# Raw FFN weights loaded two tiles ahead, the first maximum of v behind the first score tile, and the value products as one block with a priority of its own

## The chip, the cores and the metric

The kernel runs on one core of one Trainium2 chip. Five engines work side by side, each through its own queue in order: PE (TensorE, matmuls), DVE (VectorE), ACT (ScalarE), POOL (GpSimd) and SP (SyncE), which here issues all DMA transfers. The metric is device time in microseconds of one execution, the median of three runs; lower is better.

## The reference, cut to what matters

Attention in which a query sees only the keys of its own cluster, and behind it a feed-forward network (FFN) whose hidden layer is the maximum of three products. B = 4 batches, H = 8 heads, S = 768 positions, D = 64, 16 clusters; the FFN has 3072 tokens, 512 inputs and 768 hidden units. Its weights come as 8-byte floats.

```python
q_assign = np.argmax(np.einsum('bhsd,hcd->bhsc', q_n, c_n), axis=-1)
k_assign = np.argmax(np.einsum('bhsd,hcd->bhsc', k_n, c_n), axis=-1)
mask = q_assign[:, :, :, None] == k_assign[:, :, None, :]
scores = scale * np.matmul(q, k.transpose(0, 1, 3, 2))
scores = np.where(mask, scores, -1000000000.0)
scores = scores - np.max(scores, axis=-1, keepdims=True)
attn = np.exp(scores)
attn = attn / (np.sum(attn, axis=-1, keepdims=True) + 1e-09)
attn_out = np.matmul(attn, v)
...
x = attn_out.transpose(0, 2, 1, 3).reshape(B * S, H * D)
h = np.maximum(np.maximum(x @ w1, x @ w2), x @ w3)
return h @ w_out
```

## The kernel before

**Steps, visits, rounds.** The work is cut into 192 score steps: one step is one head and one block of 128 queries against all 768 keys. Six steps make a visit: a pair of heads and a group `gi` of three query blocks. Four visits, one for each pair of heads, make a round of 24 steps; two rounds make a batch. Steps 0 to 23 are the first round of batch 0.

**A score step** (`scores`, lines 477 to 496): four matmuls on PE (L482, L484), the row maximum on DVE (L487), the exponential on ACT (L490), a half-precision high part on ACT (L493) and a low part (L495, on DVE in even steps and on POOL in odd ones), and a DMA transpose issued by SP (L496), which writes the tile `pt`. The PSUM tiles `big` have three buffers, shared by scores, value products and cluster scores.

**The value products of a visit** (`av`, lines 500 to 530): first the row sums are inverted (L504 on ACT, L505 on DVE) and spread over the partitions by 12 small matmuls (L510); then come 36 matmuls of the transposed attention tiles with v (L514), in turn for the first and the second head of the pair; then the division, and a split into high and low half precision (`xs`, `x16`, L522 to L529).

**The FFN of a round** (`ffn_units`) begins three steps into the next round: 18 hidden units of 12 matmuls each (L555), then three output units of 18 matmuls each (L589), which stand under the steps 24, 25 and 26 behind the round's end. They need the weights in half precision: `w16` (six column tiles of w1, w2, w3) and `wo16`.

**The weights** are made in the first two rounds. There are 24 raw tiles of 512 KB: three for each of the six column tiles (`w_units`) and six of w_out (`wo_units`). `convert` (lines 189 to 201) takes a buffer `wd` (two of them), has SP load the raw tile (L195), casts its upper words on ACT (L197) and joins the rest on DVE (L199). Before the load, `hold` (lines 118 to 120) has POOL copy one element of the latest row sum of the exponentials (`pace`) into the buffer, so that the load waits for that exponential. For each column tile follow a maximum (L225), a scale and three splits (L208 to L210, or L205 and L206); `common` scales w_out once, at the end.

**v.** For batch 0 all of v is loaded at the start in two tiles `vf` of 768 KB. Their maxima on DVE (L314) give one scale, and `v_prep` splits v pair by pair. The first of the two maxima stands ahead of the cluster rows of the first pair, behind the low part of q and k (`behind("lo", ...)`); the second comes with the first steps.

**What sets the order.** A planner orders the instructions of each engine when the program is built, on a modelled clock: of those that are ready in the model it takes the one with the lowest priority number, and it puts in all semaphores. `at_prio` sets that number from a step number; `spread` hands units out over a range of steps, with an offset that moves their number (`W_LATE` = -2, `F_LATE` = 0, `AV_LATE` = 2, `PREP_LATE` = -9). `tc.issue_after(x)` adds no wait: it only places instructions behind x in the queue of x's engine. `behind("nm", ...)` places units behind the latest row maximum on DVE, `behind("pe", ...)` behind the latest score matmul on PE. A visit's `av` is traced one step after the next visit has begun, with the number of the visit's end + 2.

Of the kernel before, what the change touches and what calls it, by code (L numbers as in the profile page):

```python
# [8 lines left out]
F32 = mybir.dt.float32  # L9
# [3 lines left out]
I16 = mybir.dt.int16  # L13
# [11 lines left out]
def kernel(  # L25
# [90 lines left out]
    pace = []  # L116

    def hold(x):
        if pace:
            nc.gpsimd.tensor_copy(x, pace[-1])  # L120

# [67 lines left out]
    def convert(wp, src, a, d):  # L189

        n = d.shape[-1]
# [3 lines left out]
        nc.sync.dma_start(out=xf[:, 1 : 1 + 4 * n].rearrange("p (a m) -> p a m", a=a), in_=src)  # L195
        up = top[0]
        nc.scalar.copy(up.bitcast(F16).rearrange("p (n w) -> p n w", w=2)[:, 0:n, 1], x[:, 1:, 0].bitcast(BF16))  # L197
        low = x[:, 0:n, 2:4].bitcast(I32).rearrange("p n w -> p (n w)")
        nc.vector.scalar_tensor_tensor(  # L199
            d.bitcast(I32), low, 13, up[:, 0:n], op0=ALU.logical_shift_right, op1=ALU.bitwise_or  # L200
        )
# [10 lines left out]
    def w_units(wp, jt):  # L212
# [4 lines left out]
        def load(i):  # L217
            def f():
                if not i:
                    got["x"] = wp.tile([P, 3 * n], F32, tag="wf", name="wf", bufs=2)  # L220
                w = (w1, w2, w3)[i].bitcast(I16).rearrange("(c p) n -> p c n", p=P)
                src = w[:, :, 4 * jt * P : 4 * (jt + 1) * P]
                convert(wp, src, CT, got["x"][:, i * n : (i + 1) * n])
# [21 lines left out]
        return [load(i) for i in range(3)] + [scale] + [split(i) for i in range(3)]  # L245

    def wo_units(fp):
        got = []

        def part(jt):  # L250
            def f():
                wp = fp[0]
                w = w_out.bitcast(I16)[jt * P : (jt + 1) * P, :]
                if jt % 3 == 0:
                    got[:] = [wp.tile([P, 3 * DM], F32, tag="wf", name="wf", bufs=2)]
                x = got[0][:, jt % 3 * DM : (jt % 3 + 1) * DM]
                convert(wp, w.rearrange("p (a n) -> p a n", a=1), 1, x)
# [27 lines left out]
        return [part(jt) for jt in range(JT)] + [common]  # L285
# [22 lines left out]
    def v_max_first():  # L308
        def part(i):
            def f():  # L310
                x = v_first[i] = fp[0].tile([P, 2 * S], F32, tag="vf", name="vf", bufs=2)
                h = H // 2
                nc.sync.dma_start(out=x, in_=vv[0, :, i * h : (i + 1) * h].rearrange("p h t d -> p (h t d)"))
                nc.vector.tensor_reduce(  # L314
                    vmax[:, 0, i : i + 1], x, axis=AX.X, op=ALU.max, apply_absolute_value=True
                )
# [160 lines left out]
    def scores(b, h, qt, pt, g, rs, by_pool):  # L477
# [12 lines left out]
        nc.scalar.activation(x, e, AF.Exp, bias=nm, scale=-1.0, accum_out=r)  # L490
        pace[:] = [r[0:1]]
# [8 lines left out]
    def av(b, pr, gi, pts, rs):  # L500

        v = v16[b, pr]
        t = big()
        nc.scalar.activation(rs, rs, AF.Copy, bias=1.0e-9)  # L504
        nc.vector.reciprocal(rs, rs)  # L505
        for g in range(G):
            at = 512 + g * P
            for i in range(2):
                w = rs[:, g, i : i + 1].broadcast_to([P, D])
                nc.tensor.matmul(t[D * i : D * i + D, at : at + P], w, ident, start=True, stop=True)  # L510
        parts = [(kt, a, c) for a, c in ((0, 0), (1, 0), (0, 1)) for kt in range(QT)]
        for n, (kt, a, c) in enumerate(parts):
            for i in range(2):
# [6 lines left out]
                )  # L520
        xs = sb.tile([P, NB], F32, tag="xs", name="xs", bufs=1)
# [88 lines left out]
    V_0, W_0 = 2, 2  # L610


# [7 lines left out]
    W_A, W_B, W_O = (3, 27), (25, 37), (33, 47)  # L620
    AV_LAG = 2
    PREP_LATE = -9
    W_LATE, F_LATE, AV_LATE = -2, 0, 2
# [22 lines left out]

    c_sb = load_centroids()
# [6 lines left out]
    behind("lo", vm[0])  # L654
    first[5]()
    wa = [u for j in range(JA) for u in w_units(fp[0], j)]

    def unpaced(u):
        p = pace[:]
        pace.clear()  # L660
        behind("nm", u)
        pace[:] = p

    spread([lambda u=u: unpaced(u) for u in wa[:W_0]], 0, 0)
    spread([lambda u=u: behind("nm", u) for u in prep_units(0, 1)], 0, 3, -4)
    spread([lambda u=u: behind("nm", u) for u in vm[1:]] + [lambda: v_prep(0, 0, True)], 0, 4, 0)
    spread(prep_units(0, 2), 4, 9, -4)
    spread(prep_units(0, 3), 10, 15, -4)
    spread([open_late], LATE, LATE)
    for pr in range(1, NPAIR):  # L670
        spread([lambda pr=pr: v_prep(0, pr, True)], pr * V - V_0, pr * V, 0)

    spread(wa[W_0:], *W_A, W_LATE)
    spread([u for j in range(JA, JT) for u in w_units(fp[0], j)], *W_B, W_LATE)
    spread(wo_units(fp), *W_O, W_LATE)
# [23 lines left out]
    for b, pr, gi in visits:  # L699
# [9 lines left out]
        u = lambda a=(b, pr, gi, pts, rs): behind("pe", av, *a)  # L709
        plan.setdefault(step + AV_LAG - 1, []).append((step + AV_LATE, u))  # L710
# [38 lines left out]
```

## Time and profile before

| | us |
|---|---|
| median of 3 runs | 871.94 (867.68 to 874.14) |
| the profiled execution's own time | 872.91 |
| its span, first to last instruction | 871.1 |

The page lists busy times by engine, a chain of work followed back from the last instruction, and groups of instructions by source line; L487 is line 487 of the kernel printed above. "a <-b" after a group's or a wait's name is what ended the wait. In lists of waits the three numbers are the total in us, the number of waits and the longest one. In timelines they are the start and the length in us. PEld is TensorE's weight load, which runs beside the matmuls; SPq is SP's queue. Consecutive matmuls overlap, so the end of one row of PE can lie behind the start of the next one.

### The profile page before, as it was taken

How to read it: one execution, taken by the hardware profiler on the slowest of the kernel's cores; microseconds unless marked ns; L12 is line 12 of the kernel's file. 1: busy time of each engine (PE TensorE's matmuls, PEld its weight loads, DVE VectorE, ACT ScalarE, POOL GpSimd, SP SyncE). 2: the span in 40 equal slices, each digit the busy share in tenths (PEclk: the TensorE clock that was granted, in tenths of full speed). 3: DMA queues.
4: the chain of work that ended last, by engine and by line, in shares of the span. 5: the costliest groups of instructions: out<-in, count | busy, mean ns of one | idle time of the engine just before them, and what ended most of it. 6: DMA issues, size and time to landing. Idle time of an engine off the chain costs nothing.

```text
span 871.1 us, 13288 instructions
## 1 busy us (share of the span) xinstructions
PE 729.3 (84%) x4629; PEld 391.6 (45%) x4629; DVE 559.7 (64%) x1169; ACT 463.1 (53%) x827; POOL 450.4 (52%) x464
## 2 busy tenths in 40 slices
PE   2035374788868989999789999997999999999997
PEld 0012132344434545555444555454545554555563
DVE  7663877786897867547686686368768663556110
ACT  2545467654663646646554656464556465566201
POOL 1166355658585565337655745266666652354221
PEclk9976566689888999999999999999999999999999
DMA  6176869986786778768888978597986976666300
GB/s 230 36 169 140 201 143 214 203 182 139 178 204 128 171 167 154 138 117 165 170 157 201 188 139 142 113 180 144 189 194 128 156 136 134 112 118 110 91 1 36
DMA packets 329154, 128.90 MB, mean 148 GB/s; under 512 B 304384, under 2 KB 315520, under 8 KB 329088
## 3 DMA queue, kind: packets, MB, share of 16 engines
q1 hardware_dynamic: 329088, 128.06, 71.5%
q8 instruction: 36, 0.59, 0.3%
q14 instruction: 30, 0.25, 0.1%
HBM read 31.49 MB, written 6.29 MB: 43 GB/s over the span
## 4 chain that ended last, share of the span: by engine, by line
PE 45%; DVE 18%; POOL 11%; DMA 10%; issue 9%; ACT 5%; SPq 1%; POOLq 0%; DVEq 0%; ACTq 0%
PE one L555 17%; PE one L589 11%; PE big L514 7%; DVE big L487 4%; PE big L482 4%; PE big L484 3%; POOL hl L495 3%; DMA pt<-hl 2%; DMA stage<-in_qk_dram 2%; PE big L510 2%; DMA wd<-in_moe_w_dram 2%; DMA wd<-in_moe_w_out_dram 2%; POOL qk L399 2%; DMA stage<-in_v_dram 2%; DVE hl L495 2%
## 5 line engine op out<-in xcount | busy, mean ns | idle before, releaser
L487 DVE TENSOR_SCALAR_CACHE_REDUCE big<-big,nsc 128x768 f32<-128x768 f32 x192 | 194.2, 1017 | 78.3 <-PE big L484 77.1
L495 POOL TENSOR_TENSOR hl<-e,hl 128x768 f16<-128x768 f32 x96 | 159.0, 1656 | 148.9 <-ACT hl L493 147.3
L555 PE MATMUL one<-x,w16a 128*128 128x384 f16 x1152 | 208.1, 330 | 5.1 <-DVE vf_h L567 3.7
L490 ACT ACTIVATE big<-big,nm 128x768 f32<-128x768 f32 x96 | 83.8, 873 | 146.3 <-DVE big L487 130.9
L555 PEld LDWEIGHTS <-w16a 128*128 128x128 f16 x1152 | 111.1, 98 | 90.0 <-issue 21.1
L482 PE MATMUL big<-qk 128*128 128x512 f16 (+1 forms) x384 | 105.9, 357 | 48.5 <-DVE hl L495 14.0
L514 PE MATMUL big<-pt,v 128*64 128x384 f16 x1152 | 129.8, 341 | 2.4 <-DMA pt<-hl 2.4
L490 ACT ACTIVATE e<-big,nm 128x768 f32<-128x768 f32 x96 | 86.5, 901 | 71.3 <-DVE big L487 56.4
L495 DVE TENSOR_TENSOR hl<-big,hl 128x768 f16<-128x768 f32 x96 | 91.4, 952 | 41.8 <-ACT hl L493 39.6
L555 PE MATMUL one<-x,w16b 128*128 128x384 f16 x576 | 108.3, 340 | 6.7 <-DVE vf_h L567 5.2
L484 PE MATMUL big<-qk 96*128 96x512 f16 (+1 forms) x384 | 106.5, 357 | 6.9 <-DVE qk L465 4.3
L514 PEld LDWEIGHTS <-v 128*64 128x64 f16 x1152 | 71.8, 114 | 50.9 <-issue 26.0
L482 PEld LDWEIGHTS <-qk 128*128 128x128 f16 x384 | 35.6, 102 | 104.8 <-issue 67.2
L493 ACT CAST hl<-e 128x768 f16<-128x768 f32 x96 | 80.1, 834 | 2.4 <-DMA pt<-hl 0.6
L555 PEld LDWEIGHTS <-w16b 128*128 128x128 f16 x576 | 57.5, 101 | 51.3 <-issue 17.5
L493 ACT CAST hl<-big 128x768 f16<-128x768 f32 x96 | 76.6, 798 | 2.0
L528 POOL TENSOR_SCALAR x<-xs 128x384 f16<-128x384 f32 x32 | 16.4, 512 | 99.3 <-DVE xs L524 83.8
L484 PEld LDWEIGHTS <-qk 96*128 96x128 f16 x384 | 40.4, 105 | 40.0 <-issue 9.2
L589 PE MATMUL one<-wo,wf_h 128*128 128x512 f16 x216 | 56.0, 381 | 0.8 <-ACT o L598 0.8
L589 PE MATMUL one<-wo,vf_h 128*128 128x512 f16 x216 | 51.8, 380 | 2.7 <-DVE vf_h L567 2.4
L367 DVE TENSOR_REDUCE q_m<-stage 128x1 f32<-128x768 f32 x32 | 30.2, 948 | 33.9 <-DMA stage<-in_qk_dram 33.8
L399 POOL TENSOR_TENSOR qk<-stage,qk 128x768 f16<-128x768 f32 x30 | 49.6, 1667 | 3.1 <-ACT qk L398 2.9
(150 smaller groups left out, 892.5 us busy)
## 6 DMA issues: line engine op xcount, KB each, us to landing
stage<-in_qk_dram SPq DMA_DIRECT2D x32, 384.0 KB, 5.0
wd<-in_moe_w_dram SPq DMA_DIRECT2D x18, 512.0 KB, 4.8
out_dram<-o SPq DMA_DIRECT2D x24, 256.0 KB, 2.5
qk<-qk SPq DMA_DIRECT2D x15, 384.0 KB, 4.3
qk<-qk SPq DMA_DIRECT2D x30, 192.0 KB, 3.4
stage<-in_v_dram SPq DMA_DIRECT2D x12, 384.0 KB, 4.6
pt<-hl SPq DMA_TRANSPOSE x192, 4.0
wd<-in_moe_w_out_dram SPq DMA_DIRECT2D x6, 512.0 KB, 4.5
```

Of the source, the lines that this page charges most:

```text
L367: nc.vector.tensor_reduce(m2[:, i : i + 1], x, axis=AX.X, op=ALU.max, apply_absolute_value=True)
L399: last["lo"] = nc.gpsimd.tensor_tensor(t[:, AQ, i], x, t[:, BQ, i], op=ALU.subtract)
L482: nc.tensor.matmul(t[:, lo:hi], aq[:, qs], ak[:, lo:hi], start=True, stop=False)
L484: last["pe"] = nc.tensor.matmul(t[:, lo:hi], bq[0:K2, qs], bk[0:K2, lo:hi], start=False, stop=True)
L487: last["nm"] = nc.vector.tensor_scalar(e, e, nsc[b, h // 2], 3.0e38, op0=ALU.mult, op1=ALU.min, accum_out=nm)
L490: nc.scalar.activation(x, e, AF.Exp, bias=nm, scale=-1.0, accum_out=r)
L493: nc.scalar.copy(hl[:, 0, :], x)
L495: eng.tensor_tensor(hl[:, 1, :], x, hl[:, 0, :], op=ALU.subtract)
L510: nc.tensor.matmul(t[D * i : D * i + D, at : at + P], w, ident, start=True, stop=True)
L514: nc.tensor.matmul(t[D * i : D * i + D, 0:NB], v[:, i, kt, a], pts[i][:, :, c * QT + kt, :], start=(n == 0), stop=(n == len(parts) - 1),)
L555: nc.tensor.matmul(t[:, 0:NB], w16[jt // JA][:, jt % JA, wa, i, ct], x16[b, gi, ct][:, xa, :], start=(n == 0), stop=(n == 3 * CT - 1),)
L589: nc.tensor.matmul(t[:, 0:DM], h16[jt][:, ha, tt * P : (tt + 1) * P], wo16[0][:, jt, wa, :], start=(n == 0), stop=(n == 3 * JT - 1),)
```

## The change

`convert` falls into `w_load` (buffer and DMA) and `w_convert` (cast and join); `hold` and `pace` go. The 24 raw tiles are numbered in order, six column tiles first, then w_out, and tile n has the nominal step k = 2 + 1.9 (n - 2). Its load stands at k - 1, its conversion at k + 1, and the scale and splits of a column tile at k + 2 to k + 5 of its third raw tile. Each of these units is traced behind the latest row maximum, exponential and transpose (`paced`), with a number two steps earlier. The first two raw tiles are loaded at the start, ahead of and behind the second pair's q and k and the two tiles of v. The scale of w_out moves to step 47.

The two maxima of v follow behind the row maximum of step 1, their scale behind that of step 2. The preparation of the third and fourth pair of heads stands at steps 2 to 7 and 7 to 13 (before: 4 to 9 and 10 to 15), behind the latest row maximum.

`av` falls into `av_sums` (the inverted row sums and their 12 matmuls), `av` (the 36 products) and `x_split`. They are still traced one step after the next visit has begun. Sums and split keep the number of the visit's end + 2; the products have the visit's end - 4.

```diff
-        x = wp.tile([P, n + 1, 4], I16, tag="wd", name="wd", bufs=2)
-        hold(x[0:1, 0, 0:2].bitcast(F32))
...
+    def w_load(wp, src, a, n):
+        x = wp.tile([P, n + 1, 4], I16, tag="wd", name="wd", bufs=2)
...
+    def w_convert(x, d):
...
-        return [part(0), part(1), sc]
+        return [lambda: load(0), lambda: load(1), part(0), part(1), sc]
...
+    def paced(step, u, keys=("nm", "exp", "dma"), late=-2):
+
+        def f():
+            with ExitStack() as st:
+                for k in keys:
+                    st.enter_context(tc.issue_after(last[k].ins))
+                u()
+
+        plan.setdefault(max(int(step // 1), 0), []).append((step + late, f))
...
-    behind("lo", vm[0])
+    wl[0]()
     first[5]()
...
+    second = prep_units(0, 1)
+    second[0]()
+    vm[0]()
+    vm[1]()
+    wl[1]()
+
+    W_STEP = 1.9
+    for n in range(24):
+        k = 2 + (n - 2) * W_STEP
+        if n >= 2:
+            paced(k - 1, (wl + ol)[n])
+        paced(max(k + 1, 0.5), (wc + oc)[n])
+        if n < 18 and n % 3 == 2:
+            for i, u in enumerate(wu[n // 3][2]):
+                paced(k + 2 + i, u)
+    paced(47, w_common)
+    spread([lambda u=u: behind("nm", u) for u in second[1:]], 0, 3, -4)
+    spread([lambda u=u: behind("nm", u) for u in vm[2:]] + [lambda: v_prep(0, 0, True)], 1, 4, 0)
+    spread([lambda u=u: behind("nm", u) for u in prep_units(0, 2)], 2, 7, -4)
+    spread([lambda u=u: behind("nm", u) for u in prep_units(0, 3)], 7, 13, -4)
...
-        u = lambda a=(b, pr, gi, pts, rs): behind("pe", av, *a)
-        plan.setdefault(step + AV_LAG - 1, []).append((step + AV_LATE, u))
+        k = step + AV_LAG - 1
+        plan.setdefault(k, []).extend(
+            [
+                (k + 1, lambda a=(b, pr, gi, rs): behind("pe", av_sums, *a)),
+                (k - 5, lambda a=(b, pr, gi, pts): behind("pe", av, *a)),
+                (k + 1, lambda a=(b, pr, gi): x_split(*a)),
+            ]
+        )
```

More of the change, by code (lines that the diff above doesn't have):

```diff
@@ L112, in pow2_scale @@
         return p, s
[L116 to L120, printed above, removed]
     last = {}
@@ L218, in f, with conv @@
             def f():
+                w = (w1, w2, w3)[i].bitcast(I16).rearrange("(c p) n -> p c n", p=P)
+                got[i] = w_load(wp, w[:, :, 4 * jt * P : 4 * (jt + 1) * P], CT, n)
+            return f
+        def conv(i):
+            def f():
                 if not i:
                     got["x"] = wp.tile([P, 3 * n], F32, tag="wf", name="wf", bufs=2)
-                w = (w1, w2, w3)[i].bitcast(I16).rearrange("(c p) n -> p c n", p=P)
-                src = w[:, :, 4 * jt * P : 4 * (jt + 1) * P]
-                convert(wp, src, CT, got["x"][:, i * n : (i + 1) * n])
+                w_convert(got.pop(i), got["x"][:, i * n : (i + 1) * n])
                 if i == 2:
@@ L243, in split, with load, f @@
             return f
-        return [load(i) for i in range(3)] + [scale] + [split(i) for i in range(3)]
+        return [load(i) for i in range(3)], [conv(i) for i in range(3)], [scale] + [split(i) for i in range(3)]
     def wo_units(fp):
         got = []
+        raw = {}
+        def load(jt):
+            def f():
+                w = w_out.bitcast(I16)[jt * P : (jt + 1) * P, :]
+                raw[jt] = w_load(fp[0], w.rearrange("p (a n) -> p a n", a=1), 1, DM)
+            return f
         def part(jt):
             def f():
-                wp = fp[0]
-                w = w_out.bitcast(I16)[jt * P : (jt + 1) * P, :]
                 if jt % 3 == 0:
-                    got[:] = [wp.tile([P, 3 * DM], F32, tag="wf", name="wf", bufs=2)]
+                    got[:] = [fp[0].tile([P, 3 * DM], F32, tag="wf", name="wf", bufs=2)]
                 x = got[0][:, jt % 3 * DM : (jt % 3 + 1) * DM]
-                convert(wp, w.rearrange("p (a n) -> p a n", a=1), 1, x)
+                w_convert(raw.pop(jt), x)
                 row = worow[:, jt : jt + 1]
@@ L283, in common @@
             wsc["w"], wsc["o"] = pw, po
-        return [part(jt) for jt in range(JT)] + [common]
+        return [load(jt) for jt in range(JT)], [part(jt) for jt in range(JT)], common
     vmax = cpool.tile([P, B, NPAIR], F32, name="vmax")
@@ L308, in v_max_first, with load @@
     def v_max_first():
+        def load(i):
+            x = v_first[i] = fp[0].tile([P, 2 * S], F32, tag="vf", name="vf", bufs=2)
+            h = H // 2
+            nc.sync.dma_start(out=x, in_=vv[0, :, i * h : (i + 1) * h].rearrange("p h t d -> p (h t d)"))
         def part(i):
             def f():
-                x = v_first[i] = fp[0].tile([P, 2 * S], F32, tag="vf", name="vf", bufs=2)
-                h = H // 2
-                nc.sync.dma_start(out=x, in_=vv[0, :, i * h : (i + 1) * h].rearrange("p h t d -> p (h t d)"))
+                x = v_first[i]
                 nc.vector.tensor_reduce(
@@ L489, in scores @@
         r = rs[:, g, (h & 1) : (h & 1) + 1]
-        nc.scalar.activation(x, e, AF.Exp, bias=nm, scale=-1.0, accum_out=r)
-        pace[:] = [r[0:1]]
+        last["exp"] = nc.scalar.activation(x, e, AF.Exp, bias=nm, scale=-1.0, accum_out=r)
         hl = sb.tile([P, 2, S], F16, tag="hl", name="hl", bufs=4)
@@ L498, with av_sums @@
     x16 = {}
-    def av(b, pr, gi, pts, rs):
-        v = v16[b, pr]
-        t = big()
+    av_out = {}
+    def av_sums(b, pr, gi, rs):
+        t = av_out[b, pr, gi] = big()
         nc.scalar.activation(rs, rs, AF.Copy, bias=1.0e-9)
@@ L510, in av @@
                 nc.tensor.matmul(t[D * i : D * i + D, at : at + P], w, ident, start=True, stop=True)
+    def av(b, pr, gi, pts):
+        v = v16[b, pr]
+        t = av_out[b, pr, gi]
         parts = [(kt, a, c) for a, c in ((0, 0), (1, 0), (0, 1)) for kt in range(QT)]
@@ L520, in av, with x_split @@
                 )
+    def x_split(b, pr, gi):
+        t = av_out.pop((b, pr, gi))
         xs = sb.tile([P, NB], F32, tag="xs", name="xs", bufs=1)
@@ L609 @@
     QK_BUFS = 4
-    V_0, W_0 = 2, 2
     QK_LO = (1, 0, 0, 0)
@@ L645, in at_prio, with f @@
         u(*args)
+    wu = [w_units(fp[0], j) for j in range(JT)]
+    wl = [u for j in range(JT) for u in wu[j][0]]
+    wc = [u for j in range(JT) for u in wu[j][1]]
+    ol, oc, w_common = wo_units(fp)
+    def paced(step, u, keys=("nm", "exp", "dma"), late=-2):
+        def f():
+            with ExitStack() as st:
[3 more added lines that the diff above has]
+        plan.setdefault(max(int(step // 1), 0), []).append((step + late, f))
     c_sb = load_centroids()
@@ L653 @@
         u()
-    behind("lo", vm[0])
+    wl[0]()
     first[5]()
[L656 to L668, printed above, removed]
+    second = prep_units(0, 1)
[17 more added lines that the diff above has]
+    spread([lambda u=u: behind("nm", u) for u in prep_units(0, 3)], 7, 13, -4)
     spread([open_late], LATE, LATE)
     for pr in range(1, NPAIR):
[L671 to L675, printed above, removed]
+        spread([lambda pr=pr: v_prep(0, pr, True)], pr * V - 1, pr * V, 0)
     for b in range(B):
```

7 lines of the change are left out of this document (3 added, 4 removed).

## The prediction

> **What bounds the kernel now.** I read the page's busy times first, then the span cut into stages, then the chain of waits inside each stage, then the single waits.
>
> ```profile
> span 871.1 us, 13288 instructions
> PE 729.3 (84%) x4629; PEld 391.6 (45%) x4629; DVE 559.7 (64%) x1169; ACT 463.1 (53%) x827; POOL 450.4 (52%) x464
> ```
> No engine is full over the whole span, so the stages decide. Each of the 192 score steps has one row maximum on DVE (L487); first and last start:
>
> ```profile
> L487 DVE TENSOR_SCALAR_CACHE_REDUCE big<-big,nsc x192: 974/1018/1028, 24.8 to 804.8; 128x768 f32<-128x768 f32 x192
> ```
> Counted through the timeline, step 24 starts at 147 us and step 48 at 257: I cut there. Columns: busy time of each engine and its instructions, the clock granted to TensorE, the DMA share.
>
> ```profile
> core 0: us, PE busy (x) PEld busy (x) DVE busy (x) ACT busy (x) POOL busy (x), PEclk, DMA share, GB/s
> 0.00:25.00 25.00, 5.50 (x18) 2.02 (x18) 18.33 (x44) 6.35 (x12) 3.35 (x32) 1.00 0.58 201
> 25.00:147.00 122.00, 53.13 (x269) 24.26 (x268) 81.15 (x162) 68.95 (x114) 57.95 (x57) 0.71 0.71 155
> 147.00:257.00 110.00, 85.43 (x503) 46.14 (x503) 88.51 (x192) 67.17 (x121) 78.98 (x85) 0.81 0.82 179
> 257.00:805.00 548.00, 523.95 (x3478) 285.94 (x3478) 362.44 (x758) 311.29 (x565) 297.07 (x275) 0.98 0.77 150
> ```
> From 257 to 805 PE is busy 524 of 548 us at a clock of 0.98: there PE bounds the kernel, at 91 us a round of 24 steps (548 / 6). The first two rounds take 122 and 110 us with PE at 53 and 85, at a clock of 0.71 and 0.81; DVE is busiest but has 41 and 21 us idle. No engine is full there: it is a stretch of waits. The chain of waits, by line, of those two rounds:
>
> ```profile
> by line: DMA wd<-in_moe_w_dram 13.5%; issue 10.6%; DMA stage<-in_v_dram 5.3%; DMA pt<-hl 4.5%; DMA qk<-qk 4.5%; POOL v L341 4.4%; POOL qk L399 4.3%; POOL w16a L210 4.2%; DVE big L487 3.6%; ACT stage L397 3.5%; DVE q_m L367 2.9%; DVE wmx L22
> by line: DMA wd<-in_moe_w_out_dram 14.5%; issue 12.0%; PE one L555 8.9%; DVE wf L199 7.5%; DVE big L487 7.1%; PE big L514 4.9%; DMA pt<-hl 4.3%; PE big L482 3.7%; PE big L484 3.3%; POOL hl L495 3.0%; PE big L510 2.9%; DVE hl L495 2.4%; DVE
> ```
> The raw FFN weights stand at its head: their transfers are 13.5% of 122 us, 16.5 us, in the first round and 14.5% of 110 us, 16.0 us, in the second; 32 us together. The waits say how:
>
> ```profile
> DVE wf L199 <- ACT top L197: 20.3, 12, 3.6
> ACT top L197 <- DMA wd<-in_moe_w_dram: 18.4, 11, 5.3
> ACT top L197 <- DMA wd<-in_moe_w_out_dram: 10.9, 5, 5.7
> POOL wd L120 <- DVE wf L199: 8.7, 3, 4.1
> ```
> ACT takes its instructions in order, and its cast of a raw tile (L197) stood 18.4 + 10.9 = 29.3 us before a tile that had not landed. Exponentials queue behind it. DVE then waited 20.3 us for that cast (L199), and POOL's pacing copy (L120) for DVE.
>
> **The raw loads.** Before, each conversion issues its own load, held back by a one-element copy on POOL; the landing times in the two early rounds, and that of all transposes from the page:
>
> ```profile
> wd<-in_moe_w_dram SPq DMA_DIRECT2D x16, 512.0 KB, 4.6
> ...
> pt<-hl SPq DMA_TRANSPOSE x46, 4.8
> ```
>
> ```profile
> pt<-hl SPq DMA_TRANSPOSE x192, 4.0
> ```
> The change issues a load one step before its tile's nominal step and the conversion one step after it: two steps, 2 x 122/24 = 10 us, against a landing of 4.6 us. So the ACT waits should go. What is late next? In the first round DVE (81 of 122) and the DMA engines (0.71); in the second DVE (89 of 110) and DMA (0.82). Taking off all 32 us would put DVE at 170 of 200 us and the DMA share near 0.88 (the present 0.71 x 122 + 0.82 x 110 = 177 us, over 200), with the same handshakes between five in-order engines as now. The later rounds, which also hold preparation but no conversions, still need 91 us. I take half, -16 us; the ends are 0 and -32.
>
> The pacing copies go as well:
>
> ```profile
> L120 POOL COPY wd<-rs 1x1 f32<-1x1 f32 x22 | 4.6, 216 | 18.6 <-DVE wf L199 8.7 <-ACT e L490 5.8 <-DVE s_w L111 2.0
> ```
> 22 copies of 216 ns free 4.6 us of POOL. POOL is busy 58 and 79 us in these rounds, so I count nothing; end -4.6.  In place of the copies, every load, cast, scale and split stands by order alone behind the latest row maximum on DVE, exponential on ACT and transpose on SP. On SP 22 of 24 loads move about two steps forward in a queue that carries the transposes; number and size stay, and what a load holds up behind it, it held up before: 0. A load can now stand in SP for its buffer (two, as before): load n+2 comes 2.8 steps after tile n's nominal step and the conversion that frees the buffer 1 step after it, 1.8 steps or 9 us ahead, so 0 while conversions run to plan. Behind a late one the transposes of a step would queue: end +5 us, one landing. The first load now precedes the second pair's q and k; before, a value tile of 768 KB stood there instead of 512 KB: 0. The preparations of pairs 2 and 3 come two or three steps earlier, but no longer into step 0; the scale of w_out comes at step 47, and its first use follows at 48: 0, with an end of +2.
>
> **The first value maximum.** DVE on the way to the first score tile and behind it:
>
> ```profile
> 14.16 1.75 DVE L314 TENSOR_REDUCE vmax<-vf 128x1 f32<-128x1536 f32 x1
> 15.94 0.56 DVE L411 COPY qk<-qk 64x1536 f16<-64x1536 f16 x1
> ...
> 24.77 1.03 DVE L487 TENSOR_SCALAR_CACHE_REDUCE big<-big,nsc 128x768 f32<-128x768 f32 x1
> ...
> 25.82 1.81 DVE L367 TENSOR_REDUCE q_m<-stage 128x1 f32<-128x768 f32 x2
> 27.54 1.74 DVE L314 TENSOR_REDUCE vmax<-vf 128x1 f32<-128x1536 f32 x1
> ...
> 29.80 1.80 DVE L367 TENSOR_REDUCE q_m<-stage 128x1 f32<-128x768 f32 x2
> 31.52 1.02 DVE L487 TENSOR_SCALAR_CACHE_REDUCE big<-big,nsc 128x768 f32<-128x768 f32 x1
> ```
> The 1.75 us reduction at 14.16 holds the copies that follow it, and step 0 with them. Now both maxima stand behind the row maximum of step 1 (31.52), and the two reductions of pair 2 (1.80 us together) behind that of step 2. That takes 1.75 us from the way to step 0 and 1.74 + 1.80 from the way to step 1. It is work moved, not saved, and it meets the preparation of pair 1, whose ACT work follows; I take -2, ends -5.3 (all of it) and +1.75 (the first maximum ahead of something later).
>
> **The value products.** PE's timeline where the fourth pair's products meet the output products of the FFN:
>
> ```profile
> 366.22 1.67 PE L589 MATMUL one<-wo,wf_h 128*128 128x512 f16 x7
> ...
> 368.19 0.39 PE L589 MATMUL one<-wo,wf_h 128*128 128x512 f16 x1
> 368.51 0.35 PE L514 MATMUL big<-pt,v 128*64 128x384 f16 x1
> 368.80 0.39 PE L589 MATMUL one<-wo,wf_h 128*128 128x512 f16 x1
> 369.11 0.35 PE L514 MATMUL big<-pt,v 128*64 128x384 f16 x1
> ...
> 373.93 0.35 PE L514 MATMUL big<-pt,v 128*64 128x384 f16 x1
> 374.21 0.39 PE L589 MATMUL one<-wo,wf_h 128*128 128x512 f16 x1
> 374.53 2.30 PE L514 MATMUL big<-pt,v 128*64 128x384 f16 x26
> ```
> One product (L514), one output matmul (L589), in turn, eleven output matmuls and ten products between 368.19 and 374.53: 6.34 us. In the code both have the same priority number: the products of a round's fourth pair stand under the round's end + 2, and so does the third output block. Contiguous, 35 products take 3.11 us:
>
> ```profile
> 345.17 0.33 PE L514 MATMUL big<-pt,v 128*64 128x384 f16 x1
> ...
> 347.65 3.11 PE L514 MATMUL big<-pt,v 128*64 128x384 f16 x35
> ```
> That is 89 ns each, and seven output matmuls in a row took 1.67 us, 0.24 each (366.22). Eleven and ten in blocks would be 11 x 0.24 + 10 x 0.089 = 3.5 us: 2.8 us lost. Such a stretch occurs once in each of five rounds; the first is above, the last is this:
>
> ```profile
> 733.06 0.35 PE L514 MATMUL big<-pt,v 128*64 128x384 f16 x1
> ...
> 739.09 2.30 PE L514 MATMUL big<-pt,v 128*64 128x384 f16 x26
> ```
> Five times 2.8 is 14 us, in a stage where PE is the bound. The Trainium skill, "TensorEngine Tiling (Array Packing)", Key Properties, says that changing the tiling mode drains TensorE, and here 128x64 products alternate with 128x128 ones; the trace agrees, 0.60 us a pair (368.51 to 369.11) against 0.33. By the warm latency formula of "TensorE: Matmul & The Clock Gate", Single matmul latency, a fully drained pair would take 0.33 + 0.38 = 0.71 us, an estimate, and five stretches would give back about 20 us; the trace's 0.60 stands.
>
> In the change the products carry a priority six steps earlier, which nothing else then waiting has, so the planner should run them in one piece as in the second fence. The lone first product of a block (345.17) stays: it needs only the first head's transposes. The sums and the division move behind the products and keep their number. With PE at 524 of 548 us I take -12; ends 0 and -17, the latter with the few other broken blocks.
>
> What the block could wait for are the transposes:
>
> ```profile
> PE big L482 <- DVE hl L495: 4.9, 4, 2.2
> ...
> PE big L514 <- DMA pt<-hl: 1.0, 2, 0.6
> ```
> PE waited 1.0 us for them in six rounds, so the planner's idea of their landing has been late enough: 0, upper end in the rival below.
>
> **Sum.** -16 - 2 - 12 = -30 us. The profiled execution took 872.91 us (span 871.1, 1.8 around it), 1.0 over the median of 871.94, so 871.94 - 30 = 842 us.
>
> **Rivals.** *All of it comes back.* With 32 + 5.3 + 14 = 51 us off, 821 us. For it: ACT's wait costs DVE 20.3 us in turn, and both rounds end far above 91. Against: DVE would then be at 85%. 0.18.
>
> *The landings were cover.* The waits go to DVE and the handovers, and only PE's 12 us remain: 860 us. For it: POOL, DVE and ACT hand each score tile over three times, and "issue" is 10.6 and 12.0% of the chain. Against: the waits for raw tiles stand at the head of both lists. 0.15.
>
> *The block stands at the head of PE's queue and waits.* PE runs in order; with a priority before the next scores, a block placed a little too early holds scores and FFN matmuls. Transposes land in 4.0 us in the median, and one on the chain took 5.53:
>
> ```profile
> 127.14 5.53 DMA pt<-hl
> ```
> If all 32 blocks stood 1.5 us too early: 48 us, less 30 is +18, 890 us. It decides from 30/32 = 0.9 us a block. Against: the 1.0 us above. The Trainium skill, "TensorE: Matmul & The Clock Gate", Part 1, speaks against the change here: an idle window of about 3.4 us halves the clock. The granted clock of 0.71 in the first round and 0.98 later agrees with that; waits of 1.5 us would not reach it, longer ones would add to the price. 0.10.
>
> *The change does not do what it says.* The planner may issue a product only when its predecessor is done in its model, and put others between as now; conversions may wait for buffers instead of landings. Then 871 us, within 5 either way. For it: the lone first product is just such a case. Against: blocks of 35 form today beside waiting FFN matmuls of lower priority. 0.12.
>
> **How the numbers follow.** The forecast has 0.45, with its own range of 831 to 855 (8 to 24 us from the loads, 8 to 15 from the products, 1 to 2 from the start). About 1%, 9 us, is what a measurement here tells from no change. Faster by more: 0.45 + 0.18 + nearly all of the second rival, 0.77; within 1%: 0.12; slower: 0.11. The range leaves out half of the first rival below and the third above: 818 to 872.
>
> **What would show it.** Right: casts L197 without waits for wd, rounds 0 and 1 near 113 and 103 us, the first row maximum at 23 us, no alternation of L514 with L589, and output rounds some 2.5 us shorter. Wrong: L514 waiting for pt by more than 0.9 us a block; rounds 0 and 1 as long as before, with DVE or SP as the new releaser; or singles between L589 as now.

## The result, and the profile after

The changed kernel takes 866.1 us (median; 862.61 to 868.97) against 871.35 for the kernel before beside it (867.68 to 875.18): a ratio of 0.9936, with a 95% interval of 0.9918 to 0.9954. It is faster by 5 us, where 30 were forecast. The profiled execution took 865.91 us.

From the page of the changed kernel, its span and busy times:

```profile
span 864.0 us, 13260 instructions
PE 711.1 (82%) x4629; PEld 395.7 (46%) x4629; DVE 555.2 (64%) x1169; ACT 460.2 (53%) x827; POOL 448.7 (52%) x442
```

The same 4629 matmuls take 711.1 us of PE, 18.2 fewer than before. The span fell by 7.1. So PE was relieved as planned and did not turn the relief into time. The stages of the changed kernel, cut at the same steps as in the prediction (row maxima of steps 0, 24 and 48, and the last one; columns as there):

```profile
0.00:22.70 22.70, 5.36 (x17) 2.01 (x18) 16.45 (x43) 5.59 (x11) 3.34 (x32) 1.00 0.61 221
22.70:139.00 116.30, 54.31 (x273) 26.12 (x271) 80.35 (x166) 72.02 (x121) 61.42 (x52) 0.67 0.78 171
139.00:237.60 98.60, 80.67 (x511) 46.19 (x512) 80.83 (x187) 63.08 (x115) 72.86 (x69) 0.86 0.89 190
237.60:797.80 560.20, 509.51 (x3466) 288.21 (x3466) 368.24 (x760) 310.09 (x566) 297.92 (x274) 0.98 0.77 147
```

Up to step 48 the change is 19 us ahead (237.6 against 256.6). Behind it, PE's busy time fell by 14 us (523.95 to 509.51), but the stage grew from 548 to 560 us: PE now stands idle for 51 us of it, where it stood for 24. Cut by rounds, first before, then after: rounds 3 and 4, rounds 5 and 6, round 7.

```profile
358.80:541.70 182.90, 173.41 (x1157) 94.12 (x1156) 123.54 (x262) 104.58 (x190) 103.89 (x96) 0.99 0.83 161
541.70:722.90 181.20, 174.46 (x1156) 95.04 (x1155) 120.59 (x253) 105.75 (x193) 104.03 (x96) 0.98 0.78 153
722.90:804.80 81.90, 81.90 (x552) 45.59 (x551) 43.28 (x77) 46.66 (x87) 32.02 (x30) 1.00 0.67 121
```

```profile
348.40:536.70 188.30, 165.94 (x1138) 94.17 (x1136) 124.93 (x263) 103.31 (x186) 104.37 (x96) 0.97 0.79 154
536.70:719.80 183.10, 169.33 (x1156) 95.81 (x1155) 121.90 (x253) 103.56 (x190) 104.25 (x96) 0.99 0.81 151
719.80:797.80 78.00, 78.00 (x553) 44.97 (x551) 43.22 (x80) 47.88 (x89) 32.18 (x30) 1.00 0.74 127
```

Round 7 prepares no further batch (DVE does 43 us of work in it). PE is busy in all of it, and there the change brought 3.9 us. Rounds 3 to 6 hold the preparation of q and k of batches 2 and 3. There PE's busy time fell by 7.5 and 5.1 us, and the time rose by 5.4 and 1.9. The cut of rounds 3 and 4 holds 19 matmuls fewer than before (1138 against 1157): 90 output matmuls where there were 109, since more of them now run ahead of step 72. So these two rounds lost more than the 5.4 us shown. Rounds 5 and 6 hold the same 1156.

In single rounds the cuts shift still more work. The odd rounds look shorter (round 3: 93.4 to 87.9 us, round 5: 94.1 to 87.9) and the even ones, which begin with a new batch, longer (round 4: 89.5 to 100.4; round 6: 87.0 to 95.3; and round 2, 102.2 to 110.7). But rounds 3 and 5 now hold 537 and 555 matmuls where they held 569 and 570, and rounds 4 and 6 hold 602 each where they held 588. A part of this is work that changed sides, not time won or lost.

The waits of the changed kernel for raw tiles, over the whole span:

```profile
ACT top L193 <- DMA wd<-in_moe_w_dram: 17.2, 10, 4.8
DVE wf L195 <- ACT top L193: 16.2, 9, 3.7
ACT top L193 <- DMA wd<-in_moe_w_out_dram: 1.4, 1, 1.4
```

The later stage alone, before and after:

```profile
DVE q_m L367 <- DMA stage<-in_qk_dram: 26.9, 11, 3.3
DVE vmax L335 <- DMA stage<-in_v_dram: 7.8, 7, 2.1
```

```profile
DVE q_m L378 <- DMA stage<-in_qk_dram: 37.0, 14, 7.1
DVE vmax L346 <- DMA stage<-in_v_dram: 15.8, 5, 7.0
PE big L528 <- DMA pt<-hl: 7.6, 6, 1.7
```

DVE now waits 18 us longer for q, k and v of the next batch. The products (L528) wait 7.6 us for their transposes. As to their order, the fourth pair's block after reads:

```profile
354.05 0.33 PE L528 MATMUL big<-pt,v 128*64 128x384 f16 x1
354.31 0.60 PE L606 MATMUL one<-wo,wf_h 128*128 128x512 f16 x2
355.65 3.11 PE L528 MATMUL big<-pt,v 128*64 128x384 f16 x35
```

The lone first product is there as before; the singles between output matmuls are gone.

**What happens where a batch begins.** At step 96 (row maximum at 452.19 before, 436.28 after), SP's rows before, and the row maximum of step 99:

```profile
454.30 5.18 SPq L496 DMA_TRANSPOSE pt<-hl  x3
...
460.53 0.54 SPq L360 DMA_DIRECT2D stage<-in_qk_dram  x1
...
462.68 0.40 SPq L360 DMA_DIRECT2D stage<-in_qk_dram  x1
...
464.25 0.60 SPq L360 DMA_DIRECT2D stage<-in_qk_dram  x1
464.94 3.29 SPq L496 DMA_TRANSPOSE pt<-hl  x1
```

```profile
474.75 1.02 DVE L487 TENSOR_SCALAR_CACHE_REDUCE big<-big,nsc 128x768 f32<-128x768 f32 x1
```

After: SP's rows, the last scores of step 99 on PE, and DVE's rows.

```profile
447.63 0.83 SPq L371 DMA_DIRECT2D stage<-in_qk_dram  x1
448.58 4.49 SPq L506 DMA_TRANSPOSE pt<-hl  x2
...
453.93 2.58 SPq L506 DMA_TRANSPOSE pt<-hl  x1
...
457.75 0.58 SPq L371 DMA_DIRECT2D stage<-in_qk_dram  x1
...
460.74 0.59 SPq L371 DMA_DIRECT2D stage<-in_qk_dram  x1
```

```profile
459.53 0.49 PE L495 MATMUL big<-qk 96*128 96x512 f16 x2
```

```profile
451.87 0.95 DVE L378 TENSOR_REDUCE q_m<-stage 128x1 f32<-128x768 f32 x1 [2.78 <-DMA stage<-in_qk_dram]
...
461.70 0.95 DVE L378 TENSOR_REDUCE q_m<-stage 128x1 f32<-128x768 f32 x1 [4.96 <-DMA stage<-in_qk_dram]
...
465.03 0.95 DVE L378 TENSOR_REDUCE q_m<-stage 128x1 f32<-128x768 f32 x1 [1.61 <-DMA stage<-in_qk_dram]
...
466.37 1.02 DVE L498 TENSOR_SCALAR_CACHE_REDUCE big<-big,nsc 128x768 f32<-128x768 f32 x1
```

These loads are the fourth to sixth of the eight q and k tiles of batch 2, which begins here. Before, they go out with no transpose between them, 8.3, 10.5 and 12.1 us after the row maximum of step 96. After, three transposes stand between the first and the second, and the loads go out at 11.4, 21.5 and 24.5 us. SP's waits of the changed kernel from 447 to 461 us:

```profile
SPq L506 <- DVE q_m L378: 2.7, 1, 2.7
SPq L418 <- DMA qk<-qk: 0.8, 1, 0.8
SPq L417 <- POOL cl_t L451: 0.8, 1, 0.8
...
SPq L371 <- POOL stage L406: 0.2, 1, 0.2
```

The loads waited only 0.2 us for their own buffers. Between the first and the second load SP waited 3.5 us, for a transpose and for a move of q and k (L417). The rest of these 10 us went into issuing: three transposes, each of which takes SP 1.5 us in the median, and two moves fill its queue without a gap. DVE takes its instructions in order and stands at the maxima of those tiles (L378) for 9.4 us, with the row maximum of step 99 behind them: its scores were done by 460.0, and it ran at 466.4, 6.4 us later. From step 96 to 99 it took 22.6 us before and 30.1 after. Of these 7.5 us more, 2.9 are PE's work (156 matmuls in that stretch instead of 129), and 4.7 are idle time of PE. At step 48 the same stretch went from 27.3 to 32.7 us, at step 144 from 22.3 to 25.2. The Trainium skill, "DMA: Bandwidth & Descriptors", Anatomy of one DMA — SWDGE (gpsimd) path, says that DMA engines do not wait on semaphores and that any such wait happens on the issuing sequencer before dispatch. The rows of SP agree: a load that needed none of these tiles stood behind 3.5 us of such waits.

### The profile page after: what moved, and what is told of

Read it like the earlier page. It is cut to its first block, busy times and chain, and to the rows that moved or that the text cites. A ratio compares the mean times of both kernels' runs of the same rounds, so it can differ in the third digit from the quotient of the medians.

```text
span 864.0 us, 13260 instructions
## 1 busy us (share of the span) xinstructions
PE 711.1 (82%) x4629; PEld 395.7 (46%) x4629; DVE 555.2 (64%) x1169; ACT 460.2 (53%) x827; POOL 448.7 (52%) x442
## 4 chain that ended last, share of the span: by engine, by line
PE 44%; DVE 18%; POOL 11%; DMA 11%; issue 10%; ACT 5%; SPq 0%; DVEq 0%; POOLq 0%; ACTq 0%
PE one L572 19%; PE one L606 9%; PE big L528 7%; DVE big L498 5%; DMA stage<-in_qk_dram 4%; PE big L493 4%; PE big L495 3%; POOL qk L410 3%; DMA wd<-in_moe_w_dram 2%; DMA stage<-in_v_dram 2%; POOL hl L505 2%; DMA pt<-hl 2%; PE big L520 2%; DVE hl L505 1%; ACT hl L503 1%
## 5 line engine op out<-in xcount | busy, mean ns | idle before, releaser
L498 DVE TENSOR_SCALAR_CACHE_REDUCE big<-big,nsc 128x768 f32<-128x768 f32 x192 | 193.7, 1019 | 77.9 <-PE big L495 76.5
L572 PE MATMUL one<-x,w16a 128*128 128x384 f16 x1152 | 204.2, 327 | 15.0 <-DVE vpow L109 2.7
L501 ACT ACTIVATE e<-big,nm 128x768 f32<-128x768 f32 x96 | 86.6, 902 | 78.6 <-DVE big L498 72.7
L528 PE MATMUL big<-pt,v 128*64 128x384 f16 x1152 | 116.3, 337 | 9.2 <-DMA pt<-hl 9.2
L528 PEld LDWEIGHTS <-v 128*64 128x64 f16 x1152 | 75.1, 113 | 41.3 <-issue 17.2
L493 PEld LDWEIGHTS <-qk 128*128 128x128 f16 x384 | 35.9, 102 | 100.4 <-issue 72.3
L378 DVE TENSOR_REDUCE q_m<-stage 128x1 f32<-128x768 f32 x32 | 29.9, 947 | 39.5 <-DMA stage<-in_qk_dram 39.5
L606 PE MATMUL one<-wo,wf_h 128*128 128x512 f16 x216 | 50.6, 379 | 0.8 <-ACT o L615 0.8
```

Source lines behind the costliest of these rows:

```text
L378: nc.vector.tensor_reduce(m2[:, i : i + 1], x, axis=AX.X, op=ALU.max, apply_absolute_value=True)
L493: nc.tensor.matmul(t[:, lo:hi], aq[:, qs], ak[:, lo:hi], start=True, stop=False)
L498: last["nm"] = nc.vector.tensor_scalar(e, e, nsc[b, h // 2], 3.0e38, op0=ALU.mult, op1=ALU.min, accum_out=nm)
L501: last["exp"] = nc.scalar.activation(x, e, AF.Exp, bias=nm, scale=-1.0, accum_out=r)
L528: nc.tensor.matmul(t[D * i : D * i + D, 0:NB], v[:, i, kt, a], pts[i][:, :, c * QT + kt, :], start=(n == 0), stop=(n == len(parts) - 1),)
L572: nc.tensor.matmul(t[:, 0:NB], w16[jt // JA][:, jt % JA, wa, i, ct], x16[b, gi, ct][:, xa, :], start=(n == 0), stop=(n == 3 * CT - 1),)
```

## The experiments

Below, *tied* means that a visit's products carry the number of its end + 2, as the third output block does, so that the two can alternate; *untied* means any other number. In e2, e8 and e10 round 3 hardly alternates in spite of the tie (4 changes between products and output matmuls, against 21 in the kernel before); their rounds 4 to 7 do. All times of rounds and steps come from one profiled execution of each kernel, which lies up to 5 us off the median. "Step 48" is the start of its row maximum; r3+4 is from step 72 to step 120, and so on.

| kernel | median us | ratio, 95% interval | step 48 | r2 | r3+4 | r5+6 | r7 |
|---|---|---|---|---|---|---|---|
| before | 871.35 | | 256.6 | 102.2 | 182.9 | 181.2 | 82.0 |
| after | 866.10 | 0.9936 (0.9918 to 0.9954) | 237.6 | 110.7 | 188.3 | 183.1 | 77.9 |
| e1, products alone | 867.79 | 0.9957 (0.9934 to 0.9980) | 257.1 | 103.0 | 186.1 | 174.7 | 78.9 |
| e2, loads alone (tied) | 859.24 | 0.9840 (0.9787 to 0.9894) | 243.4 | 100.6 | 179.4 | 180.6 | 82.0 |
| e3, after, products at end + 1.5 | 863.08 | 0.9866 (0.9808 to 0.9925) | 247.3 | 104.9 | 184.8 | 180.7 | 78.6 |
| e4, after, raw loads unbound | 866.87 | 0.9941 (0.9911 to 0.9971) | 242.4 | 98.7 | 194.7 | 180.4 | 78.6 |
| e5, after, preparation later | 860.14 | 0.9842 (0.9793 to 0.9892) | 236.9 | 112.7 | 187.7 | 173.5 | 78.7 |
| e6, before, untied | 887.26 | 1.0149 (1.0102 to 1.0197) | 268.9 | 99.5 | 192.5 | 178.0 | 76.7 |
| e7, loads alone, untied | 861.38 | 0.9851 (0.9803 to 0.9900) | 244.1 | 106.1 | 183.0 | 179.4 | 76.5 |
| e8, after, tied | 863.40 | 0.9874 (0.9819 to 0.9928) | 244.4 | 103.8 | 183.9 | 182.8 | 82.1 |
| e9, after, no q/k preparation for batch 2 | 844.96 | 0.9699 (0.9633 to 0.9766) | 240.8 | 112.4 | 157.9 | 191.1 | 74.0 |
| e10, e9 tied | 849.08 | 0.9747 (0.9680 to 0.9813) | 243.5 | 100.3 | 169.1 | 184.6 | 82.2 |
| e11, after, q/k loads by ACT | 854.93 | 0.9793 (0.9733 to 0.9854) | 242.1 | 107.5 | 181.4 | 177.6 | 78.7 |
| e11, after, q/k loads by POOL | 862.32 | 0.9893 (0.9856 to 0.9930) | 243.9 | 105.8 | 182.9 | 181.7 | 78.6 |
| e12, before, q/k loads by ACT | 884.89 | 1.0157 (1.0114 to 1.0199) | 263.6 | 100.2 | 190.9 | 181.5 | 82.0 |
| e13, e2 with q/k loads by ACT | 861.69 | 0.9881 (0.9839 to 0.9923) | 247.1 | 96.9 | 187.3 | 181.1 | 82.0 |

### Each part alone

e1 is the kernel before with the divided `av` and its new numbers; e2 is the changed kernel with the old one:

```diff
-        k = step + AV_LAG - 1
-        plan.setdefault(k, []).extend(
...
+        u = lambda a=(b, pr, gi, pts, rs): behind("pe", av, *a)
+        plan.setdefault(step + AV_LAG - 1, []).append((step + AV_LATE, u))
```

> The kernel before with the new treatment of the value products alone (sums, products and split as three units, the products numbered six steps earlier). Theory A, the earlier number of the products costs time at the changes of batch: about 12 us slower than before, 880 to 886 us, and the time is lost after step 48. Theory B, the products gain what was forecast and the gain of the early rounds was given back because the later rounds merely begin earlier: 857 to 862 us. Theory C, the new order of the sums and the split costs the time, whatever the number: as in theory A.

> The changed kernel with the old value products: loads, conversions and start as changed, the products' sums ahead of them and the old number. Theory A: the 19 us that stand at step 48 are kept to the end, 850 to 855 us. Theory B: they are given back in the later rounds, 862 to 868 us.

Measured: the products alone bring 4 us, the loads with the first maximum alone 12 to 14, and both together 5. On top of the loads the products cost 7 us (859.24 to 866.10; the intervals lie apart). Round 7 keeps its gain in e1 (78.9 against 82.0), and step 48 keeps its own in e2 (243.4 against 256.6). The forecast gain is thus not lost in the first rounds. The new products, a gain alone, were a loss on top of the loads.

### Is it the early number, or the broken tie?

e3 gives the products of the changed kernel a number just ahead of the tie, not six steps ahead; e8 gives the tie back and leaves the division of `av` in three; e6 and e7 break the tie without any division, in the kernel before and in e2.

```diff
-                (k - 5, lambda a=(b, pr, gi, pts): behind("pe", av, *a)),
+                (k + 0.5, lambda a=(b, pr, gi, pts): behind("pe", av, *a)),
```

> The changed kernel with the products numbered half a step ahead of their old number instead of six steps: they no longer share a number with the third output block, but jump past nothing else. Theory A: the alternation is gone as in the changed kernel and the later rounds lose nothing, 840 to 850 us. Theory C (the order of sums and split costs the time): as the changed kernel, 862 to 870 us. Theory B: 862 to 870 us too.

```diff
-                (k - 5, lambda a=(b, pr, gi, pts): behind("pe", av, *a)),
+                (k + 1, lambda a=(b, pr, gi, pts): behind("pe", av, *a)),
```

> The changed kernel with the products divided into three units but numbered as before, so that they alternate with the third output block again. If the alternation guards the changes of batch: round 4 back near 90 us and 855 to 862 us in all, as with the loads alone. If the division costs the time: round 4 stays at 99 us or more, 864 to 872 us.

```diff
-    W_LATE, F_LATE, AV_LATE = -2, 0, 2
+    W_LATE, F_LATE, AV_LATE = -2, 0, 1.5
```

> The kernel before with one number changed: the value products stand half a step earlier (1.5 instead of 2), so that they no longer share a number with the third output block. Nothing is split up. If losing the alternation is what costs time at the changes of batch: rounds 3, 5 and 7 shorter by 3 to 6 us each, rounds 4 and 6 longer, in all 866 to 872 us, as the kernel with the new products alone. If the division of the unit into sums, products and split costs it: rounds 4 and 6 as before, 855 to 862 us.

> The new loads and start with the old undivided products, numbered 1.5 instead of 2. If the division of the unit costs the time: the gain of the loads (12 us) and of the broken ties (10 us) add up, 846 to 853 us. If losing the alternation costs it at the changes of batch: 858 to 866 us.

Measured: with the new loads in place, breaking the tie brought no gain in the whole time, neither with undivided products (e2 tied 859.24, e7 untied 861.38) nor with divided ones (e8 tied 863.40, e3 untied 863.08); the intervals of each pair overlap. So the forecast gain isn't there with the mildest number either. The rest of the way to the changed kernel's 866.10 is not taken apart: the interval of e3 meets that of the changed kernel only at the edge, so the number six steps early may cost some of it, and the division of `av` may cost some (e8 against e2, 4 us, intervals overlapping).

In these seven kernels round 4 follows the tie: 89.5, 89.4 and 91.6 us in the tied kernels before, e2 and e8, and 100.4, 99.0, 104.3 and 97.2 in the untied after, e3, e6 and e7. Rounds 3, 5 and 7 in sum go the other way: 270, 265 and 268 us tied, 254, 252, 258 and 251 untied. Again a part is the cut: the untied kernels hold 1085 to 1120 matmuls in rounds 3 and 5, the tied ones 1139 or 1140, and 602 to 614 in round 4 against 588 or 589. At about 0.2 us a matmul (an estimate from PE's busy time in these cuts), 4 to 11 of the 12 to 16 us of the odd rounds are work that stands elsewhere, and 3 to 5 of the 7 to 15 us of round 4. Round 7 holds the same 552 or 553 matmuls in before, e2, e8, after and e3, and there the broken tie is worth 3.3 to 4.2 us. Round 4 remains longer without the tie. e6 is slower by 1.5%, and its own loss lies in round 1 as well (124.6 us against 109.5), while ACT idles 52 us ahead of its casts, against 39: the old way of holding the loads seems to bear the other order badly. That part was not followed further.

### Are the raw tiles that still come late worth anything?

```diff
-            paced(k - 1, (wl + ol)[n])
+            paced(k - 1, (wl + ol)[n], ())
```

> The changed kernel with the raw loads no longer placed behind the latest transpose in SP's queue (their number stays). If ACT's remaining 17 us of waiting for raw tiles come from the transposes that stand ahead of the loads in SP's queue: under 8 us of such waits and 3 to 10 us off, 856 to 863 us. If DVE and the handovers bound the early rounds by now: the waits shrink and the time stays at 864 to 868 us.

Measured: with the raw loads placed behind nothing, ACT's idle time ahead of the casts falls from 22.7 to 3.1 us, and step 48 comes at 242.4 us, not before 237.6; the whole time is the same (866.87). The waits that were left cost no time of their own. What bounds the early rounds in their place was not taken apart.

### Is it the next batch's q and k?

e5 moves the preparation of every later batch by five steps in number. e9 leaves that of batch 2 out, and its scores use the q and k of batch 1, so e9 does less work; e10 is e9 with the tie back.

```diff
-    PREP_LATE = -9
+    PREP_LATE = -4
```

> The changed kernel with the preparation of the next batch's q and k numbered five steps later (-4 instead of -9). Theory D: the changes of batch (rounds 2, 4 and 6) lost time because DVE's row maxima queue behind maxima of q and k whose transfers have not landed; then fewer such waits (37 us from step 48 on in the changed kernel) and 5 to 15 us off, 851 to 861 us. Theory E: the loss comes from the third output block no longer being dealt out between the products; then the later number changes nothing there, 864 to 868 us.

```diff
     def scores(b, h, qt, pt, g, rs, by_pool):
+        b = 1 if b == 2 else b
...
-                spread(prep_units(b + 1, pr), t + 1, t + 10, PREP_LATE)
+                if b + 1 != 2:
+                    spread(prep_units(b + 1, pr), t + 1, t + 10, PREP_LATE)
```

> The changed kernel without the preparation of q and k of the third batch, whose scores use the second batch's q and k instead; round 4 then has no preparation at its start, round 6 has it as before. Theory D (DVE queues behind maxima of q and k whose loads come late): round 4 shrinks from 100 us to 84 us or less, since the products no longer alternate and nothing waits; round 6 stays at 93 to 96. Theory E (without the alternation PE's own order costs the time): round 4 stays above 94.

> The same work left out (preparation of q and k of the third batch), with the divided products numbered as before, so that they alternate with the third output block. Theory D: without late loads the alternation only costs, round 4 takes 3 us or more longer than in the run with the new number, 86 to 89 us. Theory E: round 4 is shorter than with the new number.

Rounds 3 and 4 of e9 (untied), then of e10 (tied):

```profile
353.20:511.10 157.90, 154.76 (x1096) 89.47 (x1095) 95.14 (x197) 97.19 (x178) 77.34 (x72) 1.00 0.74 139
```

```profile
343.80:512.90 169.10, 165.84 (x1125) 92.47 (x1124) 98.47 (x198) 99.67 (x184) 77.24 (x72) 1.00 0.68 130
```

The output matmuls among them, e9 first:

```profile
353.20:511.10 157.90, 18.94 (x84) 7.79 (x83) 1.00 0.74 139
```

```profile
343.80:512.90 169.10, 28.27 (x113) 10.66 (x112) 1.00 0.68 130
```

Without the preparation PE is idle for 3 us of either, and these two rounds take 11.2 us less with the tie broken (157.9 against 169.1). Not all of that is gain: 29 output matmuls stand outside e9's cut, 6.5 us at the 0.23 us that one takes there. Cut instead from the end of one output block to that of the next but one (359.8 to 528.2 in e9, 357.1 to 529.5 in e10), both hold 108 output matmuls, and e9 takes 4.0 us less for 33 products more, about 3 us of work. By both cuts, the broken tie is worth 4 to 7 us here, an estimate. With the preparation the same edit costs: 4.4 us between the row maxima (after 188.3, e8 183.9) for 20 matmuls less, 9.5 us between the output blocks (196.4 against 186.9) for 33 products more; by the same reckoning 6 to 9 us. The whole times agree in sign: e9 is 4 us faster than e10, with two executions of each that don't overlap, and the changed kernel 3 us slower than e8, within the noise. In e9 the stretch from step 96 to 99 takes 12.5 us instead of 30.1, and round 4 83.2 instead of 100.4. Round 6 of e9, which still has its preparation, keeps its loss (100.5 us). e5 is 6 us faster than the changed kernel. It takes the loss out of round 6 (95.3 to 86.5 us, for 581 matmuls instead of 602; its two loads at step 144 stand in SP's queue with no transpose between them), not out of rounds 2 and 4:

```profile
633.68 0.54 SPq L371 DMA_DIRECT2D stage<-in_qk_dram  x1
634.31 1.42 SPq L617 DMA_DIRECT2D out_dram<-o  x1
635.82 0.40 SPq L371 DMA_DIRECT2D stage<-in_qk_dram  x1
```

### Is it SP's queue?

```diff
-            nc.sync.dma_start(out=x, in_=qk[b, 2 * pr + i])
+            (nc.scalar if b else nc.sync).dma_start(out=x, in_=qk[b, 2 * pr + i])
```

Another queue than SP's issues these loads: ACT's or POOL's in the changed kernel, ACT's in the kernel before (e12) and in e2 (e13).

> The changed kernel with the loads of q and k of the later batches issued by ACT instead of SP, so that they stand behind no transpose. Theory D: the waits of DVE for q and k from step 48 on fall from 37 us to 20 or less, rounds 4 and 6 to 88 to 92 us, 846 to 856 us in all. Theory E: as the changed kernel, 864 to 868 us. A load that waits for its buffer at the head of ACT's queue would hold exponentials and could take the gain back.

> The same with POOL issuing these loads; POOL is the engine whose low part frees their buffers. Theory D: as with ACT, 846 to 856 us, less what POOL's issuing costs. Theory E: 864 to 868 us or more.

> The kernel before, with one edit: the q and k loads of batches 1 to 3 are issued by ACT instead of SP; sums and products alternate as before. Theory D (the loads are late only where the alternation of sums and products is gone, since PE's busy time covered them otherwise): nothing to gain here, round 4 stays at 88 to 92 us, 866 to 875 us in all. Rival (taking these loads out of SP's queue is worth the same 11 us in any version, and has nothing to do with the changed kernel): 858 to 863 us.

> The changed kernel's loads and first maximum with the old value products (alternating), and the q and k loads of batches 1 to 3 issued by ACT. Theory D: the alternation covers these loads, so as with the loads alone, 856 to 862 us, and the later odd rounds stay at 265 to 270 us in sum; the 855 us of the changed kernel with ACT's loads then is 4 us of products, out of 12 to 16. Rival (the products are worth nothing even where the loads are on time; the 855 us came from ACT's loads alone): 849 to 855 us here too.

e11 with ACT, the loads at step 96 (row maximum at 441.65) in ACT's queue:

```profile
440.82 0.33 ACTq L371 DMA_DIRECT2D stage<-in_qk_dram  x1
...
446.88 0.34 ACTq L371 DMA_DIRECT2D stage<-in_qk_dram  x1
...
450.07 0.33 ACTq L371 DMA_DIRECT2D stage<-in_qk_dram  x1
```

and its waits for q and k over the whole span (39.5 us in the changed kernel):

```profile
DVE q_m L378 <- DMA stage<-in_qk_dram: 26.7, 17, 3.9
```

Measured: the second and third load go out 5.2 and 8.4 us after the row maximum instead of 21.5 and 24.5, round 4 is back at 89.4 and round 6 at 85.3 us, and the kernel takes 854.93 us: 11 less than the changed kernel, and the fastest version of all that do the whole work. Its interval overlaps that of e2, so over e2 it isn't shown to be better. Through POOL's queue the gain is 4 us, at the edge of the noise. In the kernel before, the same loads by ACT bring no gain but a loss of 1.6%, most of it in round 1 (121.1 us) and in rounds 3 and 4; the 866 to 875 us expected were missed, and so were the rival's. So taking these loads off SP is no gain of its own. With e13 the products' worth can be read again: 861.69 tied, 854.93 untied, 7 us less (the intervals just overlap); with SP's loads it was 7 us more. So the runs speak for it that the sign of the products' term hangs on when q and k of the new batch arrive, though the second difference is at the edge of the noise.

**What stays open.** Even in e11, rounds 3 to 6 take 359 us against 360 in e2, for almost the same matmuls (2309 and 2314): PE is busy 4 us less and idle 3 us more. The gain is whole only where there is nothing to prepare (round 7). What else the preparation waits for was not taken apart. Round 2 is longer in the untied kernels with the new loads (104.9 to 112.7 us, but 98.7 in e4; tied 96.9 to 103.8), in e11 too. Here, too, the cut is a part of it (607 to 627 matmuls, 601 in e4; tied 596 to 603), and SP's queue is not the rest. Step 48 varies between 236.9 and 247.3 us in kernels whose first two rounds differ little, so single profiles show no more of round 2. Why e12 and e6 lose 12 and 15 us in round 1 is open as well.

## Why the prediction was wrong

**The raw loads, -16: near in size, not right in its working.** In the profile step 48 came 19 us earlier, 2 of them from the start, so the first two rounds gave 17. Rounds 0 and 1 took 116.4 and 98.7 us where 113 and 103 were named. The other kernels with these loads stand at 237 to 247, and e2 as a whole is 12 to 14 us faster, so in the whole time the term is rather -10 to -12, those 12 to 14 less the 2 of the start. A part of that can be the stretch of round 3, which hardly alternates in e2 (2.8 us a stretch in the forecast's count). "Casts without waits" was wrong: 18.6 of 29.3 us of them are left. The working took "two steps, 10 us" as the lead of a load. But the load is placed behind the transpose of an earlier step in SP's queue, and goes out only when that transpose's data is there; tile 14, for one, was issued at 142.7 us, landed at 147.8, and ACT stood ready for it. e4 shows that these remaining waits cost no time of their own. That half of the chain's 32 us came near the measured term was thus in part luck: the sum took the half without a row that gives it.

**The first maximum, -2: right.** The first row maximum starts at 22.6 us instead of 24.8.

**The products, -12: the step that failed.** Its first half held: the stretches are gone, PE's busy time behind step 48 fell by 14 us, as counted in five stretches, and round 7 gained 3.9 us where 2.5 were named. What failed is the sentence "in a stage where PE is the bound", and with it "With PE at 524 of 548 us I take -12". Where a batch is prepared, PE was as busy as that in part *because* it alternated. The time it wasted covered the loads, maxima and moves of the new batch's q and k. With the waste gone, those became the last to end: PE's idle time behind step 48 rose from 24 to 51 us, and at step 96 DVE stood 9.4 us before late tiles. On top of the loads the term came out as +7 us (e2 to the changed kernel), 19 off the forecast and the main part of the 24 us between 842 and 866. That breaking the tie gains nothing near 12 us in the whole time is shown by e3 and e7 beside e8 and e2. That it does gain where no batch is prepared, some 4 to 7 us in two rounds, is shown by e9 against e10. e11 and e13 speak for the lateness of the loads as a good part of it, not as all. How much of the 7 us is the number six steps early, or the division of `av`, stays open.

The rows for it were there. The Trainium skill, "Perfetto Trace Analysis", Identifying the Most-Contended Engine, warns that matmul busy time is a poor measure of how near TensorE is to its limit, and names the achieved FLOPs and the weight loads' share instead. The trace agrees in part: in rounds 3 and 4 that share was 94 of 183 us (0.51), and in round 7, where PE did bound the time, 45.6 of 81.9 (0.56). The stronger warning lay in the waits of the later stage: DVE's 26.9 us for q and k, which the prediction did not read because PE seemed full.

**The rivals.** "The block stands at the head of PE's queue and waits" was rightly held small: 7.6 us over the 24 blocks of the later stage, 0.3 a block against the 0.9 from which it decides. "The landings were cover" was true of the waits that were left (e4), but the loads did bring their time. "The change does not do what it says" is out: the singles are gone. None of the rivals had the products give back what they gained, and "All of it comes back" counted all 14 us of them.

## What to carry to other kernels

A busy engine bounds a stage only if its busy time is needed work: where part of it is waste (matmuls that alternate between tile shapes), list what that time covers, and look for the next batch's loads and what stands behind them, before the gain is counted. The quick test is to leave the covered work out, with and without the edit (e9 and e10): if the gain appears only then, the edit is sound and what it uncovers has to move. Before two stages are compared, count the instructions in both: a change of order moves work over the cut. Loads that need nothing from the present step don't belong in a queue between transposes that do, but moving them pays only once they are what ends last.

## What the runs showed of the hardware

The price of alternating 128x64 value products with 128x128 output matmuls is in PE's busy time, with no idle row to show it: 730.0 us busy in e8 and 711.1 in the changed kernel, for the same 4629 matmuls; behind step 48 alone, 526.0 and 509.4 us. e2 alternates too and lies between with 718.3 us, so the price is not the same in every kernel. In round 7, where PE is never idle, breaking the tie was worth 3.1 to 4.1 us of 82.0 in the kernels with the same 552 or 553 matmuls there (77.9 to 78.9 us), more than the one stretch of 2.8 us that was counted for it. The 76.5 and 76.7 us of e7 and e6 hold seven output matmuls less.

DMAs that one engine issues go out in the order of its queue, and issuing takes time of its own: in the changed kernel one of the 192 transposes took 1.5 us of SP's queue in the median and 1.3 at least, a load of q or k 0.6 in the median.
